# Linear attention into a soft mixture of experts: block columns laid out per head, every second tile's products on 64 rows per head, logits one tile earlier, six equal groups

## The chip, the cores and the metric

The program runs on one core of a Trainium2 chip. The metric is the device time of one execution in microseconds (us). PE is the matrix engine, PEld its weight loads, DVE the vector engine, ACT the scalar engine, POOL the general engine, SP the engine that issues the DMA transfers.

## The reference

Eight batches of eight heads, 576 positions, head width 64, everything float32. Attention without softmax, then a root-mean-square norm per head; its output, laid out as 4608 rows of 512, goes into a layer of 8 experts with 4 slots each, with a softmax over all rows (dispatch) and one over the 32 slots (combine).

```
kv  = einsum('bhsd,bhse->bhde', k, v)
out = einsum('bhsd,bhde->bhse', q, kv)
x   = out / sqrt(mean(out*out, -1) + 1e-6) * g_norm     # then 4608 x 512
logits = x @ phi                                        # 4608 x 32
d = exp(logits - logits.max(0)); d /= d.sum(0) + 1e-9
slot_input = d.T @ x                                    # 32 x 512
slot_out[e] = relu(slot_input[e] @ w1[e]) @ w2[e]
c = exp(logits - logits.max(1)); c /= c.sum(1) + 1e-9
result = c @ slot_out
```

## The kernel before

**Two parts.** The first part makes 36 tiles of 128 rows of x and gathers the 32 slot inputs; the second runs the experts and writes the result. All large loads share one ring of 17 slots of 1 MB (`ring`, filled by SP in the order of the program): first k, v and q of the eight batches, then the expert weights w1 and w2 (32 transfers). A weight transfer is issued when the ring slot that it takes is free again, so the first 17 weight tiles follow the attention data and the rest wait until expert 0 has used its first one (`expert_h`, L494).

**The attention part, per batch** (class `Kv`, three steps that are spread over three tiles): step 0 and step 1 multiply k by v (L138, and the odd 64 positions at L153), ACT copies the result (`kvT`, L161); step 2 (`slots`) transposes it (L165), multiplies it by g*phi (L167), and ACT copies both into the block matrix `bd` (L176, L182), 128 rows by 192 columns for each pair of heads. In `bd` the rows 0 to 63 belong to the first head of the pair and the rows 64 to 127 to the second. The 192 columns are 32 slot columns of head 0, 64 columns of head 0, 64 of head 1, 32 slot columns of head 1; what belongs to the other head is zero.

**Per tile T** (`products`, L208, or L199 for the border tile of two batches, T = 4, 13, 22, 31): four matmuls, one for each pair, of q (128 rows by 128) by `bd` (192 columns) into a tile `o` in PSUM, of which there are two. ACT then squares it (`sq`, L218), copies the slot columns (`part`, L225) and the head columns (`x`, L226).

**Per stage s** of two tiles, 2s and 2s+1 (the last two tiles are stages of their own, 17 and 18): DVE sums the squares (`mean_square`, ms, L231); in the next tile ACT makes the root (`root`, L237 and L238), DVE refines it by three small operations (`newton`, L245 to L247), POOL multiplies `part` by it (`scale_part`, L265) and then the two x tiles (`scale_x`, L256); DVE sums the parts over the heads into logits (`logits`, L270), from a table `logits_at` three tiles after the stage's last tile.

**Per group of tiles** (6, 6, 6, 6, 8, 4): DVE takes the maximum over the tiles (mx, L283); PE turns it (pm, L292); DVE takes the maximum of that, the running maximum, a diagonal matrix and alpha (gm, rmax, diag, alpha, L300 to L305; the first group has no running maximum and no alpha); PE spreads it to all rows (pb, L310); DVE and ACT make the exponentials d (L316, L317); PE adds d times x into pS, two tiles at a time (L328), and DVE rescales the running sum (acc, L335). The x tiles form a ring of 12.

**What sets the order.** Nothing is reordered: every engine runs its instructions in the order in which the loop over T writes them. For the tile T that order is: the attention step of a coming batch, pm if the group's maximum was taken in the tile before, `products(T)`, `root`, `square(T)`, d if due, the copies of T, pb, logits, `newton`, the scaling on POOL, `mean_square(T)`, two tiles of sums. After the loop come the last two stages, the sums of the last two groups and, between them, matmuls on zeros (`fill`, numbers in `LATE_FILL`).

**The second part**: `sTe` (the slot inputs, L441 and L448) feeds `expert_h` and `expert_y` (L494, L510), then the output is made from the combine weights (L534) and written in 12 transfers.

## Time and profile before

| | us |
|---|---|
| median of 3 runs | 190.5 (188.76, 190.5, 193.37) |
| the profiled execution | 188.83 |
| its span, first to last instruction | 187.1 |
| PE, PEld, DVE, ACT, POOL busy | 151.8, 108.4, 91.9, 87.5, 58.2 |
| o products L208 busy, 256 matmul instructions | 49.3 |
| mean_square L231 busy, 19 | 22.1 |
| logits L270 busy, 19 | 18.8 |
| scale_part on POOL L265 busy, 17 | 17.8 |
| scale_x on POOL L256 busy, 36 | 37.0 |
| DMA: 71.69 MB, mean | 383 GB/s |

Each float32 matmul of the program stands as two matmul instructions and two weight loads in the profile, so four matmuls of a tile are eight rows. A row of the timeline gives the start, the time from the first start to the last end, the engine, the line, the operation, out<-in, shapes and the number of instructions that it merges; in brackets stands the idle time of the engine before it and what ended it. A matmul's end in the profile contains its way through the array, so the distance from the start of one row to the start of the next tells what a piece of PE work takes from the engine.

### The profile page before, as it was taken

What the parts mean: (1) busy time and instruction counts of PE and PEld (TensorE: products, weight loads), DVE (VectorE), ACT (ScalarE), POOL (GpSimd) and SP (SyncE); (2) the same over time, 40 slices, a digit from 0 to 9 for tenths busy, and PEclk for the clock granted to TensorE, in tenths of its full rate; (3) what the DMA queues carried; (4) which work ended last, traced back from release to release, by engine and by line L of the source; (5) the groups of instructions that cost most, each with busy time, mean ns of one, the idle gap of its engine ahead of it and who ended that gap; (6) DMA issues with size and microseconds to landing.
All of it is one profiled execution on the core that took longest, in us unless ns stands there. A gap on an engine that the chain in (4) does not pass through costs nothing.

```text
span 187.1 us, 4844 instructions
## 1 busy us (share of the span) xinstructions
PE 151.8 (81%) x2018; PEld 108.4 (58%) x2019; DVE 91.9 (49%) x190; ACT 87.5 (47%) x221; POOL 58.2 (31%) x78
## 2 busy tenths in 40 slices
PE   7789999699889999987999539999966575897900
PEld 2559889587778886876878337665632222343300
DVE  1002274745882587559257994247831001653720
ACT  2036877859648668676498630022202010543600
POOL 6000658553656544836617854000000000000000
PEclk9999999999999999999999978999999759999995
DMA  5999999999999999999999992079999999899994
GB/s 203 422 429 403 420 406 420 410 417 418 415 419 415 420 403 424 415 419 420 420 419 419 417 422 124 4 284 417 415 424 419 420 426 422 347 420 392 399 415 202
DMA packets 11686, 71.69 MB, mean 383 GB/s; under 512 B 1296, under 2 KB 1424, under 8 KB 4496
## 3 DMA queue, kind: packets, MB, share of 16 engines
q1 hardware_dynamic: 11664, 71.37, 93.0%
q8 instruction: 16, 0.26, 0.6%
q14 instruction: 6, 0.05, 0.1%
HBM read 61.93 MB, written 9.44 MB: 382 GB/s over the span
## 4 chain that ended last, share of the span: by engine, by line
PE 50%; DMA 20%; DVE 16%; ACT 7%; issue 2%; SPq 0%; DVEq 0%; ACTq 0%
DMA w<-in_w_dram 17%; PE o L208 16%; PE kvp L138 8%; PE po L534 6%; PE pS L328 5%; DVE ms L231 4%; DMA kv<-in_kv_dram 4%; PE o L199 3%; DVE logits L270 3%; ACT sq L218 2%; DVE diag L302 2%; PE pY L510 2%; PE ph L494 2%; PE fill L367 2%; PE kvp L153 2%
## 5 line engine op out<-in xcount | busy, mean ns | idle before, releaser
L208 PE MATMUL o<-bd,q 128*128 128x192 f32 x256 | 49.3, 336 | 1.6 <-ACT bd L182 1.2
L208 PEld LDWEIGHTS o<-bd,q 128*128 128x128 f32 x256 | 40.8, 190 | 5.5 <-issue 2.8
L231 DVE TENSOR_REDUCE ms<-sq 128x16 f32<-128x1024 f32 (+1 forms) x19 | 22.1, 1162 | 36.1 <-ACT sq L218 36.1
L256 POOL TENSOR_TENSOR x<-x,r 128x512 f32<-128x512 f32 x36 | 37.0, 1049 | 2.3 <-DVE r L247 2.3
L265 POOL TENSOR_TENSOR part<-part,r 128x512 f32<-128x512 f32 x17 | 17.8, 1049 | 52.8 <-DVE r L247 49.4
L218 ACT ACTIVATE sq<-o 128x512 f32<-128x512 f32 x36 | 21.4, 596 | 16.8 <-PE o L208 16.5
L226 ACT COPY x<-o 128x512 f32<-128x512 f32 x36 | 21.8, 604 | 0.0
L510 PE MATMUL pY<-w,hT 128*32 128x256 f32 x256 | 17.2, 410 | 3.4 <-DMA w<-in_w_dram 1.9
L138 PE MATMUL kvp<-kv 128*64 128x64 f32 x512 | 18.4, 225 | 1.4 <-DMA kv<-in_kv_dram 1.4
L494 PE MATMUL ph<-w,sTe 128*32 128x256 f32 x256 | 16.2, 396 | 3.7 <-DMA w<-in_w_dram 3.7
L138 PEld LDWEIGHTS kvp<-kv 128*64 128x64 f32 x512 | 16.2, 138 | 5.1 <-DMA kv<-in_kv_dram 3.0
L270 DVE TENSOR_REDUCE logits<-part 128x64 f32<-128x512 f32 (+1 forms) x19 | 18.8, 990 | 0.1
L542 ACT COPY st<-po 128x768 f32<-128x768 f32 x12 | 9.4, 800 | 18.2 <-PE po L534 18.0
L534 PE MATMUL po<-logits,z 32*128 32x384 f32 x96 | 13.5, 526 | 2.5 <-DVE z L526 1.2
L510 PEld LDWEIGHTS pY<-w,hT 128*32 128x32 f32 x256 | 8.4, 116 | 11.9 <-issue 5.7
L494 PEld LDWEIGHTS ph<-w,sTe 128*32 128x32 f32 x256 | 8.2, 113 | 10.5 <-DMA w<-in_w_dram 3.1
L328 PE MATMUL pS<-x,d 128*32 128x129 f32 x288 | 12.1, 302 | 2.6 <-ACT alpha L320 2.6
L544 DVE COPY st<-po 128x768 f32<-128x768 f32 x12 | 11.1, 955 | 5.9 <-PE po L534 5.9
L502 ACT ACTIVATE h<-ph,rs 128x256 f32<-128x256 f32 x8 | 3.8, 472 | 20.6 <-PE ph L494 20.6
L225 ACT COPY part<-o 128x256 f32<-128x256 f32 x36 | 13.2, 368 | 0.0
L328 PEld LDWEIGHTS pS<-x,d 128*32 128x32 f32 x288 | 8.3, 120 | 5.7 <-POOL x L256 2.9
L534 PEld LDWEIGHTS po<-logits,z 32*128 32x128 f32 x96 | 6.2, 183 | 9.4 <-ACT st L542 4.1
(70 smaller groups left out, 135.2 us busy)
## 6 DMA issues: line engine op xcount, KB each, us to landing
w<-in_w_dram SPq DMA_DIRECT2D x32, 1024.0 KB, 18.8
kv<-in_kv_dram SPq DMA_DIRECT2D x16, 1024.0 KB, 14.9
out_dram<-st SPq DMA_DIRECT2D x12, 768.0 KB, 5.8
q<-in_qt_dram SPq DMA_DIRECT2D x8, 1024.0 KB, 14.4
kvr<-in_kr_dram SPq DMA_DIRECT2D x8, 256.0 KB, 15.1
qr<-in_qr_dram SPq DMA_DIRECT2D x4, 256.0 KB, 14.4
cst<-in_cs_dram SPq DMA_DIRECT2D x1, 64.5 KB, 6.8
```

Source lines behind the costliest of these rows:

```text
L138: nc.tensor.matmul(self.pkv[lo : lo + 64, w, g], lhsT=main[:, w, 1, c, lo : lo + 64], rhs=main[:, w, 0, c, lo : lo + 64], start=g == 0 and ...
L208: nc.tensor.matmul(o[:, r, :192], lhsT=q_sb[2 * g + i][:, r, at : at + P], rhs=bds[i][:, r], start=True, stop=True)
L218: nc.scalar.activation(sqs[s][:, T - starts[s]], o[:, :, 32:160], AF.Square, scale=0.125)
L226: nc.scalar.copy(xts[T % NX][:, :, :128], o[:, :, 32:160])
L231: nc.vector.tensor_reduce(out=mss[s], in_=sqs.pop(s).rearrange("p t j (w d) -> p (t j w) d", w=2), axis=AX.X, op=ALU.add)
L256: nc.gpsimd.tensor_tensor(out=x, in0=x, in1=r[:, i].rearrange("p (j w) -> p j w", w=2).unsqueeze(3).to_broadcast([P, 4, 2, D]), op=ALU.mult,)
L265: engine.tensor_tensor(out=part, in0=part, in1=rs_of[s].unsqueeze(3).to_broadcast([P, STAGES[s], H, NS]), op=ALU.mult)
L270: nc.vector.tensor_reduce(out=logits_all[:, starts[s] : starts[s + 1]], in_=parts.pop(s).rearrange("p t h n -> p t n h"), axis=AX.X, op=AL ...
L328: nc.tensor.matmul(pS[32 * j : 32 * j + 32], lhsT=ds[G][:, i], rhs=x[:, j], start=i == 0, stop=i == GROUPS[G] - 1)
L494: nc.tensor.matmul(ph[32 * j : 32 * j + 32], lhsT=sTe[:, (4 * e + c) * NS : (4 * e + c + 1) * NS], rhs=w1[:, c % 2, j * 256 : (j + 1) * 25 ...
L510: nc.tensor.matmul(pY[32 * j : 32 * j + 32, hf, :256], lhsT=hTs[e][:, c], rhs=w2[:, c], start=e == 0 and c < 4, stop=e == NE - 1 and c >= 4,)
L534: nc.tensor.matmul(po[:, u, : CT * NS], lhsT=z[lo : lo + 32, f * P : (f + 1) * P], rhs=cT[lo : lo + 32, k * CT * NS : (k + 1) * CT * NS], ...
```

## The change

It has four parts. First, the columns of `bd` are laid out per head: 32 slot columns and 64 head columns of head 0, then the same of head 1. Second, for each odd T except the border tiles (16 tiles of 36) the four matmuls of 128 rows by 192 columns become eight of 64 rows by 96 columns, one for each head, the two heads of a pair next to each other on the two halves of the rows and into two PSUM banks. The squares and the copies read `o` through a view that is the same for both layouts. Third, logits are made two tiles after the stage's last tile instead of three, ahead of `mean_square` of the next stage; the group's pm is written at the end of the tile after its maximum, pb one tile later, d one tile after that. Fourth, the groups are six of six tiles, `scale_part` of stage 17 goes to POOL, and the numbers of the last fills change.

```diff
-GROUPS = (6, 6, 6, 6, 8, 4)
+GROUPS = (6,) * 6
-LATE_FILL = (10, 6, 8, 4, 4)
+LATE_FILL = (14, 6, 6, 2, 2)
...
-                    self.bd[lo : lo + 64, :, 32 + lo : 96 + lo],
+                    self.bd[lo : lo + 64, :, 96 * i + 32 : 96 * i + 96],
...
     def products(T):
         g, t = divmod(T, 9)
+        o = ps.tile([P, 2, 512], F32, tag="o", name=f"o{T}", bufs=2)
+        i, at = (0, t * P) if t < 4 else (1, (t - 5) * P)
+        if t != 4 and T % 2:
+            v = o[:, :, :384].rearrange("p w (r n) -> p r w n", n=96)
+            for r in range(NPAIR):
+                for w in range(2):
+                    lo = 64 * w
+                    nc.tensor.matmul(
+                        v[:, r, w],
+                        lhsT=q_sb[2 * g + i][lo : lo + 64, r, at : at + P],
+                        rhs=bds[i][lo : lo + 64, r, 96 * w : 96 * w + 96],
+                        start=True,
+                        stop=True,
+                    )
+            return v
...
     for T in range(NT):
...
-        G = T_at.get(T)
-        if G is not None:
-            group_max_T(G)
         o = products(T)
...
+        old = ends.get(T - 2)
+        if old is not None and old < len(STAGES) - 2:
+            logits(old)
+            if (n := group_done(old)) is not None:
                 group_max(n)
                 T_at[T + 1] = n
         if s is not None:
             newton(s)
-            if s < len(STAGES) - 2:
-                scale_part(s, nc.gpsimd)
+            scale_part(s, nc.gpsimd)
             scale_x(s)
         if T in ends:
             mean_square(ends[T])
+        if T in T_at:
+            group_max_T(T_at[T])
+            pb_at[T + 1] = T_at[T]
+        if T in pb_at:
+            group_exp_PE(pb_at[T])
+            d_at[T + 1] = pb_at[T]
```

How this moves the instructions shows at three places. In the rows below the number behind a name is its stage, group, batch or tile, and the one after the underscore only tells buffers apart. First DVE, in the tiles 21 to 23, between two stages (r is `newton`). Before:

```order
L231 TENSOR_REDUCE ms10_974<-sq10_928 128x16
L316 TENSOR_TENSOR d2_990<-logits_191,pb2_972 128x192
L270 TENSOR_REDUCE logits_191<-part9_838 128x64
L245 SCALAR_TENSOR_TENSOR r110_999<-ms10_974,r010_985 128x16
L246 SCALAR_TENSOR_TENSOR r110_999<-r110_999,r010_985 128x16
L247 SCALAR_TENSOR_TENSOR r10_998<-r110_999,r010_985 128x16
L231 TENSOR_REDUCE ms11_1014<-sq11_988 128x16
L270 TENSOR_REDUCE logits_191<-part10_930 128x64
L245 SCALAR_TENSOR_TENSOR r111_1057<-ms11_1014,r011_1047 128x16
```

With the change:

```order
L286 TENSOR_REDUCE logits_191<-part9_871 128x64
L247 TENSOR_REDUCE ms10_1013<-sq10_967 128x16
L332 TENSOR_TENSOR d2_1031<-logits_191,pb2_1015 128x192
L261 SCALAR_TENSOR_TENSOR r110_1039<-ms10_1013,r010_1026 128x16
L262 SCALAR_TENSOR_TENSOR r110_1039<-r110_1039,r010_1026 128x16
L263 SCALAR_TENSOR_TENSOR r10_1038<-r110_1039,r010_1026 128x16
L286 TENSOR_REDUCE logits_191<-part10_969 128x64
L247 TENSOR_REDUCE ms11_1059<-sq11_1029 128x16
L261 SCALAR_TENSOR_TENSOR r111_1101<-ms11_1059,r011_1092 128x16
```

Before, the sum of squares of stage 11 stood ahead of the logits of stage 10, which the next `newton` followed; now the logits of a stage stand between its own `newton` and the next stage's sum of squares.

Second PE, in the tiles 14 and 15, with pm and pb of the second group (kvp4 is a product step of batch 4). Before:

```order
L208 MATMUL o14_684<-bd1_164,q3_105 128x192 x4
L138 MATMUL kvp4_708<-kv4_0_107 64x64 x16
L292 MATMUL pm1_725<-ident_144,mx1_698 32x128 x4
L208 MATMUL o15_737<-bd1_164,q3_105 128x192 x4
L310 MATMUL pb1_745<-diag1_730,ones_149 128x32
L138 MATMUL kvp4_708<-kv4_1_109 64x64 x16
```

With the change:

```order
L214 MATMUL o14_711<-bd1_164,q3_105 128x192 x4
L308 MATMUL pm1_732<-ident_144,mx1_698 32x128 x4
L138 MATMUL kvp4_744<-kv4_0_107 64x64 x16
L203 MATMUL o15_761<-bd1_164,q3_105 128x96 x8
L326 MATMUL pb1_776<-diag1_737,ones_149 128x32
L138 MATMUL kvp4_744<-kv4_1_109 64x64 x16
```

pm moved from behind the batch's first step to ahead of it, and o15 became eight matmuls of 96 columns; pb stays behind o15.

Third DVE again, around the maximum of the fifth group (tiles 32 to 35). Before:

```order
L231 TENSOR_REDUCE ms16_1352<-sq16_1330 128x16
L270 TENSOR_REDUCE logits_191<-part15_1279 128x64
L283 TENSOR_REDUCE mx4_1368<-logits_191 128x32
L245 SCALAR_TENSOR_TENSOR r116_1371<-ms16_1352,r016_1359 128x16
L246 SCALAR_TENSOR_TENSOR r116_1371<-r116_1371,r016_1359 128x16
L247 SCALAR_TENSOR_TENSOR r16_1370<-r116_1371,r016_1359 128x16
L231 TENSOR_REDUCE ms17_1378<-sq17_1362 128x8
L300 TENSOR_REDUCE gm4_1386<-pm4_1380 128x1
L301 TENSOR_TENSOR rmax0_192<-gm4_1386,rmax1_193 128x1
L302 TENSOR_SCALAR diag4_1385<-ident_144,rmax0_192 128x32
L305 TENSOR_TENSOR alpha4_1390<-rmax1_193,rmax0_192 128x1
L270 TENSOR_REDUCE logits_191<-part16_1332 128x64
```

With the change:

```order
L316 TENSOR_REDUCE gm4_1408<-pm4_1402 128x1
L317 TENSOR_TENSOR rmax0_192<-gm4_1408,rmax1_193 128x1
L318 TENSOR_SCALAR diag4_1407<-ident_144,rmax0_192 128x32
L321 TENSOR_TENSOR alpha4_1412<-rmax1_193,rmax0_192 128x1
L286 TENSOR_REDUCE logits_191<-part15_1336 128x64
L247 TENSOR_REDUCE ms16_1427<-sq16_1389 128x16
L332 TENSOR_TENSOR d4_1441<-logits_191,pb4_1429 128x192
L261 SCALAR_TENSOR_TENSOR r116_1449<-ms16_1427,r016_1436 128x16
L262 SCALAR_TENSOR_TENSOR r116_1449<-r116_1449,r016_1436 128x16
L263 SCALAR_TENSOR_TENSOR r16_1448<-r116_1449,r016_1436 128x16
L247 TENSOR_REDUCE ms17_1456<-sq17_1439 128x8
L286 TENSOR_REDUCE logits_191<-part16_1391 128x64
```

The group's gm to alpha came after the sums of squares of the stages 16 and 17; they now stand ahead of logits 15 and of both sums of squares.

More of the change, by code (lines that the diff above doesn't have):

```diff
@@ L193, in products @@
         g, t = divmod(T, 9)
-        o = ps.tile([P, NPAIR, 256], F32, tag="o", name=f"o{T}", bufs=2)
-        for r in range(NPAIR):
-            if t == 4:
+        o = ps.tile([P, 2, 512], F32, tag="o", name=f"o{T}", bufs=2)
[13 more added lines that the diff above has]
+            return v
+        o = o.rearrange("p a (b n) -> p (a b) n", b=2)
+        for r in range(NPAIR):
+            if t != 4:
+                nc.tensor.matmul(
+                    o[:, r, :192], lhsT=q_sb[2 * g + i][:, r, at : at + P], rhs=bds[i][:, r], start=True, stop=True
+                )
+            else:
                 for i in range(2):
@@ L205, in products @@
                     )
[L206 to L211 removed]
+        return o[:, :, :192].rearrange("p r (w n) -> p r w n", w=2)
     def square(T, o):
@@ L372, in soft_moe_linear_attention @@
         fill(EARLY[1 + i])
-    logits_at = {starts[s + 1] + 2: s for s in range(len(STAGES) - 3)} | {NT - 1: len(STAGES) - 3}
-    T_at, sums_at = {}, {}
+    T_at, pb_at, d_at, sums_at = {}, {}, {}, {}
     for T in range(NT):
@@ L412, in soft_moe_linear_attention @@
     root(s)
-    group_exp(G - 1)
-    scale_part(s - 1, nc.vector)
     logits(s - 1)
@@ L420, in soft_moe_linear_attention @@
     group_max(G)
-    for i in range(GROUPS[G - 1]):
-        group_sum(G - 1, i)
+    for i in todo_sums:
+        group_sum(*i)
     fill(LATE_FILL[0], 256)
```

30 lines of the change are left out of this document (10 added, 20 removed).

## The prediction

> **What bounds the kernel now.** I read the windows first, for the moment from which the transfers set the end.
>
> ```profile
> 105.00:110.00 5.00, 2.30 (x18) 1.73 (x18) 4.79 (x15) 2.23 (x7) 3.59 (x4) 1.00 1.01 419
> 110.00:115.00 5.00, 4.08 (x73) 3.82 (x74) 3.57 (x10) 0.84 (x4) 2.59 (x3) 0.66 0.72 298
> 115.00:120.00 5.00, 4.78 (x69) 3.24 (x66) 1.45 (x7) 0.40 (x2) 0.00 (x0) 1.00 0.03 10
> 120.00:125.00 5.00, 4.94 (x91) 2.87 (x92) 1.53 (x7) 0.95 (x2) 0.00 (x0) 1.00 0.47 162
> ```
> The last two figures of a row are the DMA share and GB/s. DMA runs at 419 GB/s, nearly stops for some 10 us, and starts again. At 420 GB/s the last three rows lack (122 + 410 + 258) / 420 x 5 = 9.4 us of transfer. The timeline tells why.
>
> ```profile
> 107.05 14.74 SPq L69 DMA_DIRECT2D w<-in_w_dram  x2
> 120.33 3.66 PE L494 MATMUL ph<-w,sTe 128*32 128x256 f32 x64
> ```
> SP waits 14.74 us to issue the next weight transfers: 17 weight tiles are in the ring, and the next needs the slot that `expert_h` of expert 0 frees. That begins at 120.33 us, when `sTe` is there. From then on DMA is full. So the end moves as far as the 120.33 moves, by 9.4 us at most. What sets the 120.33 is the attention part, which is no longer short of data: the question is its pace, tile for tile.
>
> There are two paces. The first is PE's, from the timeline of PE alone (start to start):
>
> ```profile
> 61.07 0.65 PE L328 MATMUL pS<-x,d 128*32 128x129 f32 x16
> 61.65 1.15 PE L138 MATMUL kvp<-kv 128*64 128x64 f32 x32
> 62.73 1.57 PE L208 MATMUL o<-bd,q 128*128 128x192 f32 x8
> 64.23 0.65 PE L328 MATMUL pS<-x,d 128*32 128x129 f32 x16
> 65.89 0.46 PE L153 MATMUL kvp<-kvr 64*64 64x64 f32 x16
> 66.28 1.57 PE L208 MATMUL o<-bd,q 128*128 128x192 f32 x8
> 67.69 0.38 PE L165 MATMUL kvp<-ident,kvT 128*128 128x128 f32 x2
> 68.44 0.43 PE L292 MATMUL pm<-ident,mx 128*32 128x128 f32 x8
> ```
> A tile o takes 1.50 us (62.73 to 64.23), or 1.41 where a matmul of the same 128x128 shape follows (66.28 to 67.69), so a change of shape costs 0.09. A batch's first step takes 1.08 (61.65 to 62.73), its second 1.08 + 0.39 = 1.47, its third 0.75 (67.69 to 68.44), two tiles of sums 0.58 (61.07 to 61.65).
>
> The second pace is a ring through ACT and DVE, seen where PE has little to do. From the timeline of all engines at the tiles 31 to 33:
>
> ```profile
> 98.05 0.60 ACT L218 ACTIVATE sq<-o 128x512 f32<-128x512 f32 x1
> 98.68 1.22 DVE L231 TENSOR_REDUCE ms<-sq 128x16 f32<-128x1024 f32 x1 [1.48 <-ACT sq L218]
> 99.94 0.31 ACT L237 ACTIVATE r<-ms,eps 128x16 f32<-128x16 f32 x1 [0.53 <-DVE ms L231]
> 100.28 0.22 ACT L238 ACTIVATE r<-r 128x16 f32<-128x16 f32 x1
> 101.61 0.62 ACT L218 ACTIVATE sq<-o 128x512 f32<-128x512 f32 x1
> 103.51 0.31 ACT L237 ACTIVATE r<-ms,eps 128x16 f32<-128x16 f32 x1 [0.54 <-DVE ms L231]
> ```
> The square of an odd tile (98.05) is summed on DVE (98.68), the root waits for that (99.94), and in ACT's queue the next square stands behind the root, the odd tile's at 101.61, and so on to the next root at 103.51. A stage can't be shorter than 103.51 - 99.94 = 3.57 us. A stage with batch work is PE's: 5.2 to 6.7 us by the prices above.
>
> **The odd tiles.** Eight matmuls of 96 columns instead of four of 192, each as two instructions, so 16 weight loads of 128 columns instead of 8. The price isn't in the trace, its parts are. Loads on the full array, and loads on 32 rows each, all of 128 columns:
>
> ```profile
> 59.58 0.30 PEld L208 LDWEIGHTS o<-bd,q 128*128 128x128 f32 x2 [0.68 <-ACT bd L182]
> ```
> ```profile
> 162.22 0.36 PEld L534 LDWEIGHTS po<-logits,z 32*128 32x128 f32 x8 [0.97 <-DVE st L544]
> ```
> Of two loads the second starts 0.11 us after the first (0.30 less its own 0.19). Eight loads on parts of the rows take 0.36 together, less than the 0.95 of eight in a row: loads on different rows overlap. I take this for the halves of 64 rows too. The products: (1.41 - 0.11) / 8 = 0.16 us for 192 columns, 0.08 for 96, shorter than a load. So a pair of halves takes 0.11, a tile 8 x 0.11 + 0.08 + 0.09 = 1.05 us instead of 1.50: 0.45 saved in each of 16 tiles, 7.2 in all, where PE sets the pace. The bounds of a tile: 16 loads in a row, without any overlap of the halves, 3.1 us (16 x (0.11 + 0.08) + 0.09), and 0.80 if the loads hide too. ACT's work is unchanged in elements; I price it at nothing more, since the copies of the slot columns already read runs of 32.
>
> **Logits ahead of the sum of squares.** This is where the gain goes. DVE works in order. Before, ms stood ahead of the previous stage's logits, and the ring ran by ACT alone. Now the logits of stage s stand between its `newton` and the ms of s+1, and they wait for POOL. The rows of DVE and POOL at tiles 14 and 15:
>
> ```profile
> 48.80 1.05 DVE L270 TENSOR_REDUCE logits<-part 128x64 f32<-128x512 f32 x1
> 49.89 0.48 DVE L283 TENSOR_REDUCE mx<-logits 128x32 f32<-128x192 f32 x1
> 50.29 0.17 DVE L245 SCALAR_TENSOR_TENSOR r<-ms,r 128x16 f32<-128x16 f32 x1
> 50.70 0.18 DVE L247 SCALAR_TENSOR_TENSOR r<-r,r 128x16 f32<-128x16 f32 x1
> 50.92 0.29 DVE L300 TENSOR_REDUCE gm<-pm 128x1 f32<-128x128 f32 x1
> 51.04 1.05 POOL L265 TENSOR_TENSOR part<-part,r 128x512 f32<-128x512 f32 x1 [1.83 <-DVE r L247]
> 51.24 0.86 DVE L301 TENSOR_TENSOR rmax<-gm,rmax 128x1 f32<-128x1 f32 x1
> 52.14 0.99 DVE L302 TENSOR_SCALAR diag<-ident,rmax 128x32 f32<-128x32 f32 x1
> 53.12 1.21 DVE L231 TENSOR_REDUCE ms<-sq 128x16 f32<-128x1024 f32 x1
> 53.27 0.38 PE L310 MATMUL pb<-diag,ones 128*128 128x32 f32 x2 [0.93 <-DVE alpha L305]
> ```
> The new ring: root 0.55 (99.94 to 100.49) and 0.03, `newton` 0.59 (50.29 to 50.88), 0.16 until POOL starts, its 1.05, 0.03, logits 1.07, ms 1.22, 0.04: 4.7 us instead of 3.57. The maximum mx in front of ms adds 0.4 (5.1). In a group's next stage gm, rmax, diag and alpha stand there as well; rmax and diag are held until POOL's instruction of the moment ends (51.24 + 0.86 = 52.10, POOL's at 52.09), so it is 2.24 from the end of `newton` (50.88) to the next DVE work (53.12), and the stage takes 0.58 + 0.59 + 2.24 + 1.07 + 1.22 + 0.04 = 5.7. In the first group only diag stands there, within POOL's 1.05.
>
> The waits of PE for mx go, since mx is taken a tile earlier; but pb waits for alpha, 2.39 after the end of `newton` (53.27), and that moves only as far as `newton` does. So the wait at pm turns into a longer one at pb.
>
> **The sum.** From the root of stage 0 to that of stage 15 there are 15 steps, each the longer of ring and PE (two tiles with their extras). PE decides four: stage 4, 1.08 + 1.50 + 1.47 + 1.05 + 0.58 = 5.7; stage 7, 1.47 + 1.41 + 0.75 + 1.05 + 0.58 = 5.3; stage 11, 5.7 + 0.58 = 6.3; stage 13, as 4, 5.7. The ring decides the rest: 0, 1, 3, 10 with 4.7, the stages 2, 5, 8, 14 with mx 5.1, 6, 9, 12 with alpha 5.7. Sum: 23.0 + 18.8 + 20.4 + 17.1 = 79.3 us. The copies of the block matrices on ACT come on top:
>
> ```profile
> 18.62 0.31 ACT L237 ACTIVATE r<-ms,eps 128x16 f32<-128x16 f32 x1
> 20.93 0.76 ACT L176 COPY bd<-kvp 64x256 f32<-64x256 f32 x2
> 22.25 0.60 ACT L218 ACTIVATE sq<-o 128x512 f32<-128x512 f32 x1
> ```
> They take 1.32 (20.93 to 22.25) once per batch, ahead of the root or of the odd square. In stage 0, o2 ends at 19.2, its square and copies hold ACT to 20.5, the block copies to 21.8; the square of tile 3 and its sum follow to 23.7, 5.5 after the root instead of 4.7. Going on like this they lengthen the steps of the stages 0, 4, 7 and 13 by 0.8, 0.4, 0.7 and 0.4, and elsewhere PE's lead takes 0.5 off: +1.8; bounds 0 and 7 x 1.32 = 9.2. The value is near the lower end because most copies fall while DVE is in the ring. The first root moves from 18.62 to 18.2 (one odd tile). So the root of stage 15 is at 18.2 + 79.3 + 1.8 = 99.3, before 99.94: 0.6 gained, of 7.2 + the waits at pm.
>
> The tail:
>
> ```profile
> 110.92 3.23 PE L328 MATMUL pS<-x,d 128*32 128x129 f32 x64 [2.60 <-ACT alpha L320]
> 113.05 0.38 DVE L283 TENSOR_REDUCE mx<-logits 128x32 f32<-128x128 f32 x1
> 114.08 1.26 PE L367 MATMUL fill<-zeros 128*128 128x256 bf16 x10
> 115.28 0.42 PE L292 MATMUL pm<-ident,mx 128*32 128x128 f32 x8
> 117.87 1.09 PE L328 MATMUL pS<-x,d 128*32 128x129 f32 x32
> ```
> Before, mx of the last group ended at 113.43, 13.49 after the root of stage 15, but pm stood behind the fills and came at 115.28. With the change, counted from that root: `newton` 1.17, alpha 3.41, logits 15 4.5, ms 16 5.7, `newton` 16 6.9, then POOL's part 8.1, two x 10.2, part 17 (new on POOL, half as long) 10.7, logits 17 11.3, `newton` 18 11.9, its part and logits 13.0, mx 13.5. As late as before; but the sums of the fifth group (6 tiles instead of 8) and 14 fills are done long before, and pm follows mx at once: 1.85 gained. The last group has 6 tiles instead of 4, 48 instructions at 1.09 / 32 instead of 32: 0.55 lost. Fills behind pm are covered by DVE and ACT as before. So the 120.33 moves by 0.6 + 1.85 - 0.55 = 1.9, say 2.0 us with the roundings. The profiled execution was 188.83 and becomes 186.8; the median of the runs shown stands 1.7 above it, and I forecast **188.5 us** for the median.
>
> **The rivals.** *The ring alone* (0.19): the block copies cost nothing, 1.8 more is gained: 186.7. For it: copies and ring use different engines; against it: ACT works in order. *PE decides* (0.14): if POOL's part is there before DVE needs it, the steps are PE's sums: 4.7, 2.5, 5.1, 4.0, 5.7, 4.9, 4.3, 5.3, 4.8, 5.4, 3.1, 6.3, 4.0, 5.7, 4.9, together 70.7, and over 9.4 us would be gained: the cover of the DMA ends there, 181.1. Against it: POOL starts only 0.16 after `newton`. *The copies stand in the ring in every batch* (0.08), on ACT between root and odd square: up to 9.2 - 1.8 = 7.4 more, 195.9, slower; it decides from 2.0 us of it on. *The halves don't share the array* (0.03): an odd tile takes 3.1, PE decides 13 steps, 18.8 us more, 207; slower than before from about 1.35 us a tile. *Loads wait for the products of their own rows* (0.05): a pair takes 0.11 + 0.08 = 0.19 and a tile 1.61; eight steps of PE grow by 3.7 together: 192.2. In the rows above eight loads hide behind products on the same 128 rows (1.41 for 8 x 0.16 and one load), which speaks against it. [...] *The clock drops in the tail* (0.04): PE has nothing between the fills and pm for some 3.5 us. After a wait of that kind the window 110 to 115 shows the clock at 0.66, and 64 sums took 3.23 where 32 take 1.09: 48 would take 0.8 longer, with pm and pb 1.0, 189.5. [...]
>
> **How the numbers follow.** The forecast keeps 0.47, its own range 186.7 to 190.5 (copies from 0 to 3.8). What a measurement of this kernel can tell from no change is about 2%, here 186.7 and 194.3. Faster: PE decides 0.14, half of the ring alone 0.10, 0.04 of the forecast's spread: 0.28. Slower: copies 0.07, halves 0.03: 0.10. Same: 0.62. The range for 8 in 10 takes in most of the ring alone, part of the way to PE's pace, and the waiting loads with some of the copies: 184.0 to 193.0.
>
> **What would show it.** Right: odd tiles 1.05 us start to start; logits on DVE waiting for POOL's part, and ms directly behind; stages without batch work of 4.7 us (before 3.57); PE waiting at pb and no longer at pm; pm of the last group within 0.1 of mx; `expert_h` at 118.4. Wrong: ms never behind a waiting logits, or stages of under 4.2 us without batch work; `expert_h` under 116 or over 121; an odd tile over 1.3.

## The result, and the profile after

The changed kernel takes **199.03 us** (median of 4 runs, 197.76 to 200.57), the kernel before 189.63 beside it (4 runs, 188.48 to 193.37): ratio 1.052, interval 1.038 to 1.066. It is slower by 5%; 188.5 with a range up to 193.0 was predicted. Some executions of the kernel before take 191 to 194 us instead of about 189, so every ratio here is of undisturbed executions of both kernels, of which run 6 below has too few for one. The profiled execution took 200.21, its span is 198.4 (187.1 before).

The granted clock is seen first. This is its line in the 40 slices of the page, before:

```profile
PEclk9999999999999999999999978999999759999995
```

After:

```profile
PEclk9999999759978999997599788899999755569995
```

One slice is 4.7 and 5.0 us. Before, the clock fell in the tail of the attention part (110.1 to 113.6), in the output (147.7 to 154.5) and behind the last matmuls. After, it falls five times before `expert_h` (37.0 to 43.8, 57.5 to 60.9, 91.6 to 98.5, 112.1 to 115.5, 122.3 to 125.8) and for 20.5 us in the output. The windows of the first fall, in stage 4, in steps of 3.40 us (the columns are busy time of PE, PEld, DVE, ACT and POOL, the clock, the DMA share and GB/s):

```profile
30.20:33.60 3.40, 2.61 (x29) 2.45 (x26) 2.00 (x5) 3.39 (x10) 2.58 (x3) 1.00 1.01 407
33.60:37.00 3.40, 1.81 (x27) 1.23 (x25) 2.68 (x7) 2.62 (x9) 1.26 (x2) 1.00 1.04 417
37.00:40.40 3.40, 2.96 (x36) 2.81 (x37) 3.00 (x6) 1.56 (x5) 2.25 (x3) 0.50 1.01 422
40.40:43.80 3.40, 3.40 (x28) 2.96 (x28) 1.29 (x3) 0.96 (x3) 2.94 (x3) 0.50 1.01 412
```

In the second row PE is busy for 1.81 of 3.40 us at full clock; in the two that follow it runs at half. The rows of PE there:

```profile
33.92 0.43 PE L308 MATMUL pm<-ident,mx 128*32 128x128 f32 x8
34.28 1.14 PE L203 MATMUL o<-bd,q 64*128 64x96 f32 x16
37.44 0.60 PE L326 MATMUL pb<-diag,ones 128*128 128x32 f32 x2 [2.02 <-DVE diag L318]
37.97 1.98 PE L138 MATMUL kvp<-kv 128*64 128x64 f32 x32
39.88 2.93 PE L214 MATMUL o<-bd,q 128*128 128x192 f32 x8
42.73 1.64 PE L138 MATMUL kvp<-kv 128*64 128x64 f32 x32
44.30 0.46 PE L153 MATMUL kvp<-kvr 64*64 64x64 f32 x16
44.69 1.14 PE L203 MATMUL o<-bd,q 64*128 64x96 f32 x16
45.76 0.43 PE L344 MATMUL pS<-x,d 128*32 128x129 f32 x8
```

PE waits 2.02 us for pb. What it does next takes nearly twice its price: a batch's first step 1.91 us from start to start (1.08 before), a tile 2.85 (1.50). From pb to the next odd tile, o11 (44.69), it is 7.25 us. The clock is full again from 43.8, and o11 takes 1.07 (44.69 to 45.76).

The ring of logits and the sum of squares is as the prediction drew it. ACT, DVE and POOL in stage 1:

```profile
25.07 0.31 ACT L253 ACTIVATE r<-ms,eps 128x16 f32<-128x16 f32 x1 [0.53 <-DVE ms L247]
26.07 0.17 DVE L263 SCALAR_TENSOR_TENSOR r<-r,r 128x16 f32<-128x16 f32 x1
26.39 1.05 POOL L281 TENSOR_TENSOR part<-part,r 128x512 f32<-128x512 f32 x1 [2.44 <-DVE r L263]
27.48 1.06 DVE L286 TENSOR_REDUCE logits<-part 128x64 f32<-128x512 f32 x1 [1.23 <-POOL part L281]
28.45 1.21 DVE L247 TENSOR_REDUCE ms<-sq 128x16 f32<-128x1024 f32 x1
29.69 0.31 ACT L253 ACTIVATE r<-ms,eps 128x16 f32<-128x16 f32 x1 [1.58 <-DVE ms L247]
```

Logits wait 1.23 us for POOL's part, the sum of squares comes right behind, and the stage takes 29.69 - 25.07 = 4.62 us. (What a stage takes is counted from its root to the next stage's root.) The waits of PE moved as predicted too. The rows give the total in us, the number of times and the longest one. Before:

```profile
PE pm L292 <- DVE mx L283: 4.6, 4, 1.7
PE pb L310 <- DVE alpha L305: 3.5, 5, 0.9
```

After:

```profile
PE pb L326 <- DVE alpha L321: 8.1, 4, 3.2
PE pm L308 <- DVE mx L299: 3.1, 1, 3.1
PE pb L326 <- DVE diag L318: 2.0, 1, 2.0
```

In the loop PE waits at pb and no longer at pm: in four of five groups 2.0 to 3.2 us (2.0, 2.1, 2.2 and 3.2), in the other 0.6, where 0.9 was the longest. The one wait at pm is the last group's. That tail, from the timeline:

```profile
111.87 0.39 PE L326 MATMUL pb<-diag,ones 128*128 128x32 f32 x2 [3.19 <-DVE alpha L321]
112.08 2.90 PE L214 MATMUL o<-bd,q 128*128 128x192 f32 x8
116.36 13.96 SPq L69 DMA_DIRECT2D w<-in_w_dram  x2
122.01 0.48 DVE L299 TENSOR_REDUCE mx<-logits 128x32 f32<-128x192 f32 x1
122.55 0.66 PE L308 MATMUL pm<-ident,mx 128*32 128x128 f32 x8 [3.13 <-DVE mx L299]
125.95 1.53 PE L344 MATMUL pS<-x,d 128*32 128x129 f32 x48
128.86 1.50 PE L508 MATMUL ph<-w,sTe 128*32 128x256 f32 x24 [0.28 <-DVE sTe L455]
```

pm follows mx by 0.06 us, as predicted, and `expert_h` begins at 128.86. SP still waits for it (13.96 us), so the rest of the weights is issued only then. In the output the clock is at half again. Its windows, and its first 48 matmuls, nearly all of them at half clock:

```profile
156.00:163.00 7.00, 5.38 (x48) 1.94 (x48) 0.45 (x1) 0.47 (x1) 0.00 (x0) 0.53 1.01 419
163.00:170.00 7.00, 5.21 (x32) 2.47 (x30) 0.95 (x3) 0.16 (x1) 0.00 (x0) 0.50 0.90 375
170.00:177.00 7.00, 7.00 (x36) 3.03 (x32) 3.72 (x4) 3.65 (x5) 0.00 (x0) 0.50 0.69 285
168.15 9.99 PE L548 MATMUL po<-logits,z 32*128 32x384 f32 x48 [0.61 <-DVE z L540]
```

In the kernel before, at full clock, the same 48 matmuls go from 158.44 to 165.81: 7.37 us instead of 9.99.

**Where the 11.3 us of span are**: root 0 is at 19.56 instead of 18.62 (+0.9); from root 0 to root 15, at 108.29, it is 88.73 us instead of 81.32 (+7.4); from there to `expert_h` 20.57 instead of 20.39 (+0.2); from `expert_h` to the end 69.5 instead of 66.8 (+2.8). The first of these need not be the change's: the clock became full at 9.7 us instead of 4.3, and the same happens between two executions with the same beginning (runs 8 and 9 below). Of the last of them, 2.6 are those 48 output matmuls.

**The share of the time in which PE streams.** By the clock records of the two profiles, the low stretches that end within a profile last 3.41, 6.83 or 20.48 us in the change, and 3.41 or 6.83 before; those at full clock between them last 6.83 to 30.72, and 27.31 and 34.13 before. All are whole multiples of 3.413 us. So I cut the span into windows of 3.41 us, counted from where a fall begins. For each I estimated from the rows of the trace the share of the time in which any matmul streams columns (0.16 us for 192 columns, the prediction's price; half of that per column in bf16, 0.107 for 256, where the 18 fills of run 1 take 1.96 from their start to pb's, 0.109 each; twice at half clock, where a batch's first step takes 1.91 for 1.08; products that overlap count once). In the window ahead of the falls in stages 4, 6, 13 and 15 it is 0.34, 0.21, 0.27 and 0.02, and 0.09 in the tail; the next lowest one after 10 us and before `expert_h` is 0.59. Before, the windows with the waits at pm and pb have 0.47, 0.49 and 0.53. Three explanations were tested against each other:

- **the clock** (theory A): the longer wait at pb leaves the window too empty, the clock falls to half, and the batch's products and the next tiles behind the wait run at half speed;
- **the ring** (B): the 4.6 us of logits and the sum of squares carry the loss, and the clock only falls because PE waits anyway;
- **the odd tiles** (C): being shorter, they empty the windows even where pb stands as before. (In the runs 6 and 8 C says that they don't pay.)

### The profile page after: what moved, and what is told of

Read it like the earlier page. It is cut to its first block, busy times and chain, and to the rows that moved or that the text cites. A ratio compares the mean times of both kernels' runs of the same rounds, so it can differ in the third digit from the quotient of the medians.

```text
span 198.4 us, 5102 instructions
## 1 busy us (share of the span) xinstructions
PE 160.9 (81%) x2144; PEld 113.8 (57%) x2145; DVE 95.4 (48%) x189; ACT 87.1 (44%) x221; POOL 58.7 (30%) x79
## 4 chain that ended last, share of the span: by engine, by line
PE 41%; DVE 21%; DMA 18%; ACT 9%; issue 4%; POOL 3%; POOLq 0%; DVEq 0%; SPq 0%
DMA w<-in_w_dram 16%; PE kvp L138 8%; PE po L548 8%; PE o L214 7%; DVE ms L247 5%; DVE logits L286 4%; POOL part L281 3%; PE fill L383 3%; DVE diag L318 3%; DMA kv<-in_kv_dram 2%; PE pY L524 2%; PE pS L344 2%; PE o L203 2%; DVE rmax L317 2%; PE ph L508 2%
## 5 line engine op out<-in xcount | busy, mean ns | idle before, releaser
L281 POOL TENSOR_TENSOR part<-part,r 128x512 f32<-128x512 f32 (+1 forms) x18 | 18.4, 1023 | 62.9 <-DVE r L263 60.3
L214 PE MATMUL o<-bd,q 128*128 128x192 f32 x128 | 29.0, 377 | 1.5 <-issue 0.8
L234 ACT ACTIVATE sq<-o 128x512 f32<-128x512 f32 x36 | 21.5, 598 | 13.5 <-PE o L214 9.6
L214 PEld LDWEIGHTS o<-bd,q 128*128 128x128 f32 x128 | 24.1, 219 | 3.3 <-issue 1.7
L138 PE MATMUL kvp<-kv 128*64 128x64 f32 x512 | 22.9, 257 | 0.8 <-DMA kv<-in_kv_dram 0.8
L138 PEld LDWEIGHTS kvp<-kv 128*64 128x64 f32 x512 | 20.5, 168 | 5.3 <-issue 3.0
L203 PE MATMUL o<-bd,q 64*128 64x96 f32 x256 | 18.4, 284 | 0.0
L548 PE MATMUL po<-logits,z 32*128 32x384 f32 x96 | 16.7, 684 | 1.9 <-DVE z L540 1.2
L203 PEld LDWEIGHTS o<-bd,q 64*128 64x128 f32 x256 | 15.8, 190 | 2.4 <-issue 0.5
L548 PEld LDWEIGHTS po<-logits,z 32*128 32x128 f32 x96 | 7.7, 241 | 10.8 <-ACT st L556 4.7
L383 PE MATMUL fill<-zeros 128*128 128x256 bf16 (+1 forms) x47 | 12.3, 410 | 1.2 <-DVE zeros L92 1.2
```

The source lines that it names most:

```text
L138: nc.tensor.matmul(self.pkv[lo : lo + 64, w, g], lhsT=main[:, w, 1, c, lo : lo + 64], rhs=main[:, w, 0, c, lo : lo + 64], start=g == 0 and ...
L203: nc.tensor.matmul(v[:, r, w], lhsT=q_sb[2 * g + i][lo : lo + 64, r, at : at + P], rhs=bds[i][lo : lo + 64, r, 96 * w : 96 * w + 96], star ...
L214: nc.tensor.matmul(o[:, r, :192], lhsT=q_sb[2 * g + i][:, r, at : at + P], rhs=bds[i][:, r], start=True, stop=True)
L234: nc.scalar.activation(sq, o[:, :, :, NS:], AF.Square, scale=0.125)
L281: engine.tensor_tensor(out=part, in0=part, in1=rs_of[s].unsqueeze(3).to_broadcast([P, STAGES[s], H, NS]), op=ALU.mult)
L548: nc.tensor.matmul(po[:, u, : CT * NS], lhsT=z[lo : lo + 32, f * P : (f + 1) * P], rhs=cT[lo : lo + 32, k * CT * NS : (k + 1) * CT * NS], ...
```

## The experiments

Each is told with its edit and compared with the kernel before on the same chip. Fills are matmuls on zeros; late fills stand in the second part (run 7). The median of all executions of the kernel before was 192.98 beside the runs 1 to 4, 193.05 beside 5 to 8 and 191.51 beside 9 to 11, so the ratio tells more than a median set against the first row. By the rule that a difference counts from 2% on, only the change itself is clearly slower; the runs 1 to 5 and 7 are unclear, and 8 to 11 the same as before.

| run | median, us (range) | ratio, interval | root 0 to root 15 | `expert_h` |
|---|---|---|---|---|
| before | 189.63 (188.48 to 193.37) | | 81.3 | 120.3 |
| the change | 199.03 (197.76 to 200.57) | 1.052, 1.038 to 1.066 | 88.7 | 128.9 |
| 1 change, fills ahead of pb | 193.07 (191.44 to 194.17) | 1.024, 1.006 to 1.042 | 82.8 | 122.7 |
| 2 odd tiles alone | 193.70 (193.00 to 194.05) | 1.028, 1.022 to 1.034 | 81.7 | 121.7 |
| 3 order and groups alone | 196.60 (194.34 to 198.80) | 1.040, 1.021 to 1.059 | 85.9 | 126.1 |
| 4 change, sum of squares first | 194.65 (193.60 to 196.55) | 1.032, 1.021 to 1.043 | 78.7 | 122.2 |
| 5 as 1, narrow fills | 193.92 (192.94 to 194.51) | 1.015, 1.006 to 1.024 | 83.1 | 123.2 |
| 6 as 2, fills ahead of pm, pb | 191.94 (187.08 to 192.83) | | 80.5 | 119.7 |
| 7 before, late fills | 190.06 (189.03 to 192.55) | 1.001, 0.993 to 1.008 | 81.3 | 120.3 |
| 8 as 6, late fills | 189.47 (188.72 to 190.20) | 0.993, 0.988 to 0.998 | 80.4 | 120.4 |
| 9 as 8, fills fitted | 187.82 (186.81 to 188.11) | 0.988, 0.984 to 0.993 | 78.3 | 118.8 |
| 10 odd tiles but two, late fills | 189.19 (186.75 to 193.32) | 0.992, 0.987 to 0.997 | 83.1 | 124.2 |
| 11 as 1, late fills | 192.29 (191.82 to 193.34) | 1.014, 1.009 to 1.019 | 82.8 | 122.9 |

The last two columns are us of the profiled execution, which in the runs 3 and 10 is the slowest of its kernel.

**1. The change, with something to stream while PE waits for pb.** 18 matmuls on zeros into free columns of pb's PSUM tile, in the loop.

```diff
-    def group_exp_PE(G):
-        pbs[G] = ps.tile([P, NS], F32, tag="m", name=f"pb{G}")
+    def group_exp_PE(G, warm=0):
+        t = ps.tile([P, 512], F32, tag="m", name=f"pb{G}")
+        for _ in range(warm):
+            nc.tensor.matmul(t[:, 256:], lhsT=zeros[:, :P], rhs=zeros[:, :256], start=True, stop=True)
+        pbs[G] = t[:, :NS]
...
-            group_exp_PE(pb_at[T])
+            group_exp_PE(pb_at[T], 18)
```

> The changed kernel with 18 matmuls on zeros (256 columns, bf16) written into a free part of pb's PSUM tile, ahead of pb in each of the five groups that are not the last; nothing else differs. Theory A (the granted clock: PE's waits at pb grew from about 0.9 us to 2 us and more, the clock falls to half, and batch products and o tiles behind them run at half speed): the clock stays near 1.0 from 20 to 110 us, the steps of stages 4 and 13 fall from 9.1 us to about 6, expert_h begins at about 120 instead of 128.9, time about 190. Rival B (the longer ring through POOL and DVE alone): clock or not, the steps stay, time 197 to 199.

The clock stays full until 113.8 us. Its line of the page, and PE in stage 4:

```profile
PEclk9999999999999999999999985999999965599985
33.19 1.14 PE L203 MATMUL o<-bd,q 64*128 64x96 f32 x16
35.22 2.12 PE L327 MATMUL pb<-zeros 128*128 128x256 bf16 x18 [0.89 <-DVE rmax L312]
37.18 0.31 PE L329 MATMUL pb<-diag,ones 128*128 128x32 f32 x2
37.41 1.15 PE L138 MATMUL kvp<-kv 128*64 128x64 f32 x32
38.49 1.57 PE L214 MATMUL o<-bd,q 128*128 128x192 f32 x8
```

pb comes no earlier, but the products behind it take 1.08 and 1.50 again, and from pb to o11 it is 4.29 us (41.47, by the same view) instead of 7.25. Stage 4 takes 6.93 us instead of 9.06, stage 13 6.14 instead of 9.17, and root 0 to root 15 82.8 instead of 88.7: 5.9 of the 7.4 us were the clock. The median is 6.0 us lower and the ratio 1.024 instead of 1.052. The ring is untouched (stage 1 takes 4.62 in both), so it cannot be all of the loss; 1.5 us of the 7.4 are left, 0.8 of which are the fills of stage 4: diag is done at 36.22 there and pb starts 0.96 later, against 0.15 in the change.

**2. The odd tiles alone**: the order, groups and fills of before, with the layout per head and the halves.

```diff
-GROUPS = (6,) * 6
-LATE_FILL = (14, 6, 6, 2, 2)
+GROUPS = (6, 6, 6, 6, 8, 4)
+LATE_FILL = (10, 6, 8, 4, 4)
...
+        G = T_at.get(T)
+        if G is not None:
+            group_max_T(G)
         o = products(T)
...
```

> The kernel before, with its order and its groups, and only the columns of bd laid out per head and the odd tiles on 64 rows. Theory A: PE's wait in a group's stage stays split in two of about 0.9 us (pm and pb), the clock holds in the attention part, six stages that PE decides are 0.45 us shorter each: 185 to 188. Rival B: the same, 185 to 188. Rival C (the products on 64 rows are themselves what lets the clock fall, since they put less work into the array): clock falls in the attention part here too, time 193 to 198.

193.70. The stages 2, 3, 8 and 11 gain 0.8, 0.4, 0.4 and 0.8 us against before (5.78, 4.64, 5.26 and 7.37 there), 2.4 together, and the stages 4 and 13 lose 1.6 and 1.2 (8.26 for 6.67, 8.75 for 7.59). PE in stage 4:

```profile
34.24 0.42 PE L308 MATMUL pm<-ident,mx 128*32 128x128 f32 x8 [1.27 <-DVE mx L299]
34.60 1.14 PE L203 MATMUL o<-bd,q 64*128 64x96 f32 x16
36.09 0.38 PE L326 MATMUL pb<-diag,ones 128*128 128x32 f32 x2 [0.36 <-DVE diag L318]
36.40 1.78 PE L138 MATMUL kvp<-kv 128*64 128x64 f32 x32
38.11 2.52 PE L214 MATMUL o<-bd,q 128*128 128x192 f32 x8
```

No wait here is over 1.27 us, and the clock falls all the same: the shorter tile between two short waits leaves a share of 0.35 (0.34 ahead of stage 13). So the odd tiles let the clock fall by themselves, as rival C has it; theory A, which put the fall down to the longer wait at pb alone, missed with its 185 to 188. Between the roots the kernel is no faster than before (81.7 and 81.3). Of the 4.2 us of span over before, 2.8 stand behind `expert_h`, in a part that the edit does not touch; the clock is at half there from 149.3 to 169.8.

**3. The order and the groups alone**: full odd tiles in the changed kernel.

```diff
-        if t != 4 and T % 2:
+        if False:
```

> The changed kernel, but the odd tiles with four matmuls of 192 columns like the even ones (the columns per head, the order and the six groups stay). Theory A: PE is busy 0.45 us longer ahead of each pb, so the wait there is some 1.5 us instead of 2; the clock may fall in one or two of the four groups: 190 to 196. Rival B: ring unchanged, about 197 to 199 or more. Rival C: no fall of the clock at all, about 189 to 190.

196.60, between the ranges of A and B: slower too, with one fall between root 0 and root 15 (after a window of 0.31, stage 13) and the ring's 4.6 in the stages 1 and 3 (4.62 and 4.66). Of 10.0 us of span over before, 4.6 are between these roots and 4.2 behind `expert_h`. Both parts of the change lower the share: between these roots the clock falls in stage 13 with the order, in the stages 4 and 13 with the odd tiles, and in the stages 4, 6 and 13 with both. The order and the groups were not tried apart.

**4. The sum of squares ahead of the waiting logits**, the rest as in the change.

```diff
         old = ends.get(T - 2)
+        if T in ends:
+            mean_square(ends[T])
...
-        if T in ends:
-            mean_square(ends[T])
```

> The changed kernel, but on DVE the sum of squares of a stage stands ahead of the logits of the stage before it, as in the kernel before (logits still one tile earlier than there). Theory A: the short stages are back at 3.6 us, the maximum comes 1.2 us later and PE waits for it at pm again; whether the clock falls depends on the wait at pb, which still needs newton and alpha: 190 to 196. Rival B: all of the loss is the ring, so it goes: at most 189.

The ring is gone: stage 1 takes 3.58, the clock stays full to 102.4, and root 0 to root 15 takes 78.7 us, 2.6 less than before. Then the tail takes it all back:

```profile
103.15 0.60 PE L326 MATMUL pb<-diag,ones 128*128 128x32 f32 x2 [1.61 <-DVE alpha L321]
103.56 2.91 PE L214 MATMUL o<-bd,q 128*128 128x192 f32 x8
106.40 2.03 PE L203 MATMUL o<-bd,q 64*128 64x96 f32 x16
115.80 0.44 PE L308 MATMUL pm<-ident,mx 128*32 128x128 f32 x8 [3.87 <-DVE mx L299]
```

The last two tiles run at half clock, and the last pm comes 17.2 us after root 15 (98.57; 14.3 in the change): `expert_h` is at 122.2. Rival B's 189 at most did not come, 194.65 lies in A's range. The ring is real, and worth some 3.3 us between the roots where the clock does not fall (82.8 in run 1, less the 0.8 by which its fills run over in stage 4, against 78.7 here).

**5. As 1, the fills on 32 of the 128 columns of the array.**

```diff
-            nc.tensor.matmul(t[:, 256:], lhsT=zeros[:, :P], rhs=zeros[:, :256], start=True, stop=True)
+            nc.tensor.matmul(t[:32, 256:], lhsT=zeros[:, :32], rhs=zeros[:, :256], start=True, stop=True)
```

> As the run with 18 zero matmuls ahead of pb in the changed kernel, with the same number, the same 256 columns and the same time on PE, but each on 32 of the 128 columns of the array instead of all. Theory A1 (the clock follows the work done in the array, rows times columns times streaming, over windows of 3.4 us, and falls after a window with less than about a third of the full work): the narrow ones add a quarter of the work, the clock falls again in the stages 4 and 13 and behind pb of the second group, and expert_h begins at 125 to 129. Rival A2 (the clock follows the time in which PE streams at all): no fall in the attention part, expert_h at 121 to 123 as with the wide ones.

```profile
36.19 2.12 PE L327 MATMUL pb<-zeros 128*32 128x256 bf16 x18 [0.90 <-DVE rmax L312]
```

A quarter of the array does as well: no fall until 116.8, the stages 4 and 13 take 7.11 and 6.12 (113.8, 6.93 and 6.14 in run 1). In these two runs the clock held as long with fills on 32 columns as with fills on 128.

**6. The odd tiles of run 2 with 10 fills ahead of each pm and each pb** in the loop.

```diff
-    def group_max_T(G):
-        pm = ps.tile([P, P], F32, tag="m", name=f"pm{G}")
+    def group_max_T(G, n=0):
+        t = ps.tile([P, 512], F32, tag="m", name=f"pm{G}")
+        warm(t, n)
+        pm = t[:, :P]
...
-            group_max_T(G)
+            group_max_T(G, 10)
...
-            group_exp_PE(G)
+            group_exp_PE(G, 10)
```

> The order and the groups of the kernel before, columns per head and odd tiles on 64 rows, and ten wide zero matmuls ahead of each pm and each pb in the loop. Theory A: with the clock held, what the odd tiles save is left: the stages 4 and 13 take about 6.2 and 7.2 us instead of 8.3 and 8.8, the root of stage 15 is 2.5 to 3.5 us earlier than before after its first tile, 186 to 190 depending on the clock in the output. Rival C (the odd tiles don't pay): root of stage 15 as far from the first tile as before (87.4 us), 189 to 193.

No fall in the loop; the stages 4 and 13 take 7.27 and 7.09 (8.26 and 8.75 without fills), `expert_h` begins at 119.7. But root 15 is only 0.8 us closer to root 0 than before (80.5 and 81.3), where theory A expected 2.5 to 3.5, and the median of 191.94 is in rival C's range. In the profiled execution the clock is low in the output from 154.4 to 168, and its part behind `expert_h` is 4.4 us longer than before's; one run took 187.08. Run 8 tests the output, run 9 the loop.

**7. The kernel before, with fills where the last experts wait for weights**: 8 matmuls on zeros ahead of each half of the first products of the last three experts, and of their second products in the first half.

```diff
+    def late_warm(e, c):
+        t = ps.tile([P, 2, 512], F32, tag="m", name=f"warm{e}_{c}")
+        for _ in range(8):
+            nc.tensor.matmul(t[:, 0, :256], lhsT=zeros[:, :P], rhs=zeros[:, :256], start=True, stop=True)
...
+            if e >= NE - LATE and c % 2 == 0:
+                late_warm(e, c)
```

> The kernel before, with eight wide zero matmuls ahead of each half of the last three experts' first products and of their second products, where PE waits for weights; nothing else. Theory (the spread of this kernel's times comes from the clock in the output: the first half's 48 output matmuls take about 7 us at full clock and 10 at half): the clock is full when the output begins in every run, the times gather at 187 to 189.5. Rival (the spread comes from the transfers or the attention part): the times stay spread from 188 to 193.5.

The fall in the output is gone from the profiled execution. The window of before:

```profile
147.00:154.00 7.00, 4.88 (x44) 1.91 (x48) 0.45 (x1) 0.47 (x1) 0.00 (x0) 0.55 1.01 420
```

And of this kernel:

```profile
147.00:154.00 7.00, 7.00 (x87) 4.02 (x80) 0.89 (x2) 0.95 (x2) 0.00 (x0) 1.00 1.01 419
```

The time is that of before, 1.001: the fall of 6.8 us in the profiled execution of before cost nothing that can be measured, and DMA was at 1.01 with it and without. Where it lasts longer, as in the change, it reaches the output matmuls, and the DMA share of the last window is 0.69. The ten executions take 189.03 to 192.55: not gathered below 189.5, as the theory expected, and not spread to 193.5, as the rival did. What spreads this kernel's times stays open.

**8. Runs 6 and 7 together.**

```diff
+            if e >= NE - LATE and c % 2 == 0:
+                late_warm(e, c)
...
+            if hf == 0:
+                late_warm(e, 4)
             expert_y(e, hf)
```

> The two together: order and groups of before, odd tiles on 64 rows, zero matmuls ahead of pm and pb in the loop and in the waits of the last three experts. Theory A: 184 to 187 in all runs, 1 to 2 % under the kernel before at its best. Rival C: 188 to 190.

All ten runs lie between 188.72 and 190.20, where 19 runs of the kernel before beside it lie between 188.68 and 194.25. That is rival C's range; theory A's 184 to 187 missed. Low clock is left only at 111.0 to 114.4 and behind the last matmul. The ten fills are too many in places: stage 4 takes 7.27 (6.67 before), stage 9 6.27 (5.63). The next run tests whether this is what eats the gain.

**9. As 8, the fills counted to fit the gap that each stands in.**

```diff
-            group_max_T(G, 10)
+            group_max_T(G, (8, 3, 0, 7, 10)[G])
...
-            group_exp_PE(G, 10)
+            group_exp_PE(G, (2, 10, 6, 10, 10)[G])
```

> The kernel of the eighth run, with the fills ahead of pm and pb fitted to the gap that each stood in: 8, 3, 0, 7, 10 ahead of pm and 2, 10, 6, 10, 10 ahead of pb, instead of 10 everywhere. Theory (the clock follows the share of a window in which TensorE streams; fills that outlast their gap cost what they run over): no fall of the clock before 105, the steps of the stages 4, 6, 9 and 10 shorter by 0.2 to 0.6 each than in the eighth run (7.27, 6.99, 6.27, 4.38), root 15 at 98.5 (99.62 there), expert_h at 119.2 (120.37 there), and a median of 188.4 (189.47 there). Rival (the odd tiles' gain is given back in the loop whatever the fills): root 15 within 0.3 of 99.6 and 189.5.

187.82, all six runs from 186.81 to 188.11, ratio 0.988 (0.984 to 0.993): the lowest of all, though 1.2% is less than the 2% that counts, and the interval overlaps that of run 8, which ran on another chip. The stages 4, 6, 9 and 10 take 6.60, 6.69, 5.63 and 3.92, and root 0 to root 15 78.3 us, 3.0 less than before; root 15 is at 98.05 and `expert_h` at 118.8, close to what the theory had (98.5 and 119.2). The first clock rise came late in this execution: batch 0 runs at half clock until 10 us, its first step taking 1.98,

```profile
5.70 1.98 PE L138 MATMUL kvp<-kv 128*64 128x64 f32 x32 [0.92 <-DMA kv<-in_kv_dram]
```

and that of run 8, whose program is the same up to there, at full clock:

```profile
5.77 1.15 PE L138 MATMUL kvp<-kv 128*64 128x64 f32 x32 [0.99 <-DMA kv<-in_kv_dram]
```

The clock became full at 5.2 us there and at 10.0 here. The first tile o comes 1.4 us later for it (14.14 and 12.73), and root 0 0.6 later (19.76 and 19.18); no run tells whether it can be steered.

**10. Full tiles in the two places where run 2 lost the clock** (tiles 9 and 27), no fills in the loop, late fills.

```diff
-        if t != 4 and T % 2:
+        if t != 4 and T % 2 and T not in (9, 27):
```

> The order and the groups of before, the odd tiles as halves except in the tiles 9 and 27, no fills in the attention part, and the fills of the eighth run ahead of the last experts' products. Theory: the clock fell in the stages 4 and 13 because the shorter odd tile stood ahead of the wait at pb in the same clock window; with the full tile there the window's share stays over 0.38, the clock at full before 105, the steps of the stages 4 and 13 are those of before (6.7 and 7.6, against 8.26 and 8.75 with the halves), those of 2, 3, 8 and 11 keep their gain (4.98, 4.2, 4.82, 6.62), so that root 15 comes 78.9 after root 0 (81.3 before) and expert_h 2.4 earlier: 117.9 and 186.7. Rival (the falls in the stages 4 and 13 come from elsewhere, from the layout or from the phase of the windows): one of the two steps stays over 8, root 15 is 80.5 or more after root 0, and 188.5 or more.

13 runs spread from 186.75, the expected time, to 193.32, which is the profiled one, so that the trace shows the worst of them. In it the rival's signs are there: stage 13 takes 9.52, root 15 is 83.1 after root 0, and the median is 189.19. Stage 4 takes 6.24 without a fall, as the theory has it. Stage 6 loses the clock after a window of 0.35, around another odd tile, and stage 13 after one of 0.40, with a stall in the middle of a tile that no other run shows:

```profile
91.94 0.46 PE L203 MATMUL o<-bd,q 64*128 64x96 f32 x3
93.51 1.02 PE L203 MATMUL o<-bd,q 64*128 64x96 f32 x13 [1.11 <-issue]
```

So full tiles in these two places do not keep the clock up by themselves.

**11. The change with the clock held up in the loop and in the output** (runs 1 and 7 together).

```diff
+            group_exp_PE(pb_at[T], 18)
...
+            if e >= NE - LATE and c % 2 == 0:
+                late_warm(e, c)
```

> The first run (the changed kernel with fills ahead of pb) and the fills of the eighth run ahead of the last experts' products: the change with the clock held up both in the attention part and in the output. Theory (of the change's loss the clock is the larger part, the ring of logits and the sum of squares the rest): no fall in the output, the part behind expert_h 66.7 as before (68.7 in the first run), expert_h as in the first run at 122.7, 191.1: still slower than before's 189 by 2. Rival (the clock is all of it): 189 or less.

192.29, ratio 1.014: no fall in the output, but only 0.8 us less than run 1 and 1.2 more than expected. So holding the clock up takes back 6.7 us of the median and brings the ratio from 1.052 to 1.014, which is 70 to 75% of the change's loss. It is 4.5 us above run 9, which has the same odd tiles, a clock held up as well, and the order and the groups of before: between the roots it takes 82.8 us against 78.3. So the order and the groups cost something of their own. In the tail the clock is still at half from 114.2 to 121.0.

## Why the prediction was wrong

**The step that failed is the sum's prices for PE.** They are prices at full clock: "A stage with batch work is PE's: 5.2 to 6.7 us by the prices above", and the stages 4 and 13 with 5.7 each. They took 9.06 and 9.17, with the products behind pb at half clock; with the clock held, in run 1, 6.93 and 6.14. The prediction had the pieces: that the wait at pm turns into a longer one at pb, that the odd tile is 0.45 shorter, and that the clock was at 0.66 from 110 to 115 before, around the wait of 2.60 us that ended at 110.92. It priced the last in the tail alone, at 1.0 us and a chance of 0.04. In the loop it cost 5.9, behind gaps shorter than the 3.5 us that it looked at in the tail: 2.0, 2.1 and 2.2 us in the change, and in run 2 1.27 and 0.36 around a short tile.

That the share would go down could have been worked out from the trace of before. There the window from 31.6 to 35.0, in stage 4, has 0.47 by the working above. A full tile streams for 8 x 0.16 = 1.28 us; a halved one, whose pairs overlap, for about 8 x 0.08 = 0.64. That alone takes 0.19 of a window away (run 2 has 0.35 there), and the longer wait comes on top. What that trace could not tell is the share at which the change's falls would begin: its one fall before `expert_h` stood behind a window of 0.05, and the lowest without a fall has 0.4.

**Right, point by point.**

- The odd tile: 1.05 predicted, 1.07 measured, start to start. Its loads overlap: 16 of 0.19 us each, 3.0 in a row, take 0.97 together (the odd tile at 24.72 in the change).
- The ring: 4.7 for a plain stage, 4.62 to 4.67 measured in run 1; with mx 5.1, 5.18 to 5.23; with alpha 5.7, 5.62 to 5.72; stage 0 with the copies 4.7 + 0.8, 5.58.
- The stages by PE with the clock at full, in run 1: stage 7 with its copies 5.3 + 0.7, 5.98 measured; stage 13 5.7 + 0.4, 6.14; stage 11 6.3, 6.48; stage 4 5.7 + 0.4, 6.93, where the 18 fills run 0.8 over. From root 0 to root 15 the walk had 81.1 and run 1 has 82.8; 0.8 are those fills, and 0.5 are "PE's lead", which was not there.
- pm behind mx by 0.06 (within 0.1 predicted), PE waiting at pb and no longer at pm.

**Wrong beside the clock, in size.** From root 15 to `expert_h` 19.1 was worked out and 20.57 measured: the last mx ended 14.2 after root 15 instead of 13.5, and what follows it took 6.37 instead of 5.6, at half clock from 122.3 to 125.8 (the rival's 1.0). The end behind `expert_h` was taken as it stood and is 2.8 longer, at half clock in the output; the late fills take a part of that away (67.4 from `expert_h` to the end in run 11, 68.7 without them in run 1). That no rival with the clock in the loop was on the list is why the range missed: with the clock held up in the loop and in the output, run 11's 192.29 lies inside it, still 3.8 over the forecast.

## What to carry to other kernels

In this case a shorter matmul and a longer wait did the same thing: both lowered the share of the time in which PE streams (in stage 4, 0.47 before, 0.35 with the odd tiles alone, 0.34 with the change), and what followed ran at half clock, a batch's first step in 1.91 us instead of 1.08. Before costing an edit that shortens TensorE work or moves a wait onto it, see how long the shortest low stretch of the granted clock is in the trace (3.41 us here), work out the streaming share of each window of that length around the place, and hold the lowest one against the lowest that the trace shows without a fall. Matmuls on zeros, counted to fit the gap and no more, kept the clock up here (1.00 from 30 to 50, 80 to 100 and 148 to 176 us in run 9): from run 2 to run 9, with such fills in the loop and in the output, the median went from 193.70 to 187.82, and root 0 to root 15 from 81.7 to 78.3.

## What the runs showed of the hardware

From the time at which it was first full to `expert_h`, the clock fell to half behind each of the 22 windows whose share I estimate at 0.35 or less in thirteen profiles (0.02, 0.09, 0.21, 0.27 and 0.34 in the change, 0.05 before, 0.34 and 0.35 in run 2, 0.31 in run 3, 0.35 in run 10, among others), once behind 0.40 (run 10), and behind no other; the lowest shares without a fall are 0.38, 0.39 and, before, 0.41. The share is my own estimate from the rows, single values move by some hundredths with its details, and the numbers say no more than where the falls of these profiles stood. Fills on zeros kept the clock at full in stage 4 (run 1, 6.93 us instead of 9.06), and so did fills on a quarter of the array (run 5, 7.11). Ahead of `expert_h`, the falls of the change and of before that lasted one window had that window, at half clock, filled to 0.77 to 0.85 by the same estimate; the two that lasted two, in the stages 4 and 13 of the change, had the first filled to 0.65 and 0.69. In the change's output the clock was at half until 176.96, though PE was busy all the time from 170.
